# An attention and MoE chain on one core: the order in which weight units are converted, and how many by the end of the attention

## The chip, the cores and the metric

The kernel runs on one core of a Trainium2 chip. Its engines are TensorE (PE, matrix products; its weight loads are shown apart as PEld), VectorE (DVE), ScalarE (ACT), GpSimd (POOL) and SyncE (SP), which here issues the transfers. Each takes its instructions in the order of its own queue. The metric is the time of one execution on the device, in microseconds.

## The reference

A local attention with a few global keys, and then two feed-forward layers ("MoE" by name, with a single expert each) on its output, all in fp32:

```python
scores = scale * (q @ k.T) + bias          # 2 batches x 8 heads, 768 tokens, head size 64
a = softmax(where(keep, scores, -1e9))     # keep: 8 global keys, 96 local ones behind each token
x = (a @ v) as 1536 tokens x 512
h = x @ w_in                               # 512 -> 2048
y = (h * tanh(softplus(h))) @ w_out        # 2048 -> 512
h2 = y @ w2_in
out = softplus(h2) @ w2_out
```

## The kernel before

**Products in two parts.** A factor of a MoE product is held as two float32r tiles, a rounded one and the rest, and a product takes three passes: rounded with rounded, rounded with rest, rest with rounded. The weights arrive as 64-bit words. One **unit** is half a weight tile: 128 partitions x 512 words. A transfer on SP brings its raw words (0.5 MB, `fetch`, line 194), three DVE instructions of `widen` make fp32 of them (lines 145, 150 and 154, into a buffer `a`, with a PSUM bank `bits` between), ACT casts that to the rounded part (line 209), and POOL subtracts it from `a` for the rest (line 211). Unit part 0 of tile n holds the columns that the up product of chunk n needs, part 1 the rows for its down product. There are 16 tiles of a layer, so 64 units in two layers; `raw` and `a` have two buffers each, and the fetch of unit u+2 is issued behind the widening of unit u.

**The order of units** is the list `units` (line 173). Per layer it runs over the tiles: part 0 of tile f, then part 1 of tile f-3 (`SKEW`). Units 10, 11, 12 and 13 so are the second half of tile 3, the first of 7, the second of 4 and the first of 8. The first seven tiles (`EARLY`) live in pool `wa`, which is there from the start; tiles 7 to 14 live in `wb`, which is opened at line 347 behind the attention and lies over memory that the attention's tiles held. A unit of tile 7 can be cast only when these have been read for the last time.

**The attention** works in 24 steps (two query tiles of two heads each): scores on PE (`sp`, line 462), scores with bias and their maximum on DVE (481), exponentials on ACT (492), a small scaling of the sums on POOL (501), the reciprocal on DVE (503), normalisation on POOL (506), transposes on PE (522) and their copies on ACT or DVE (525), products with the values on PE (`xhalf`, 539), and the split of the result into x on ACT and DVE (553, 554). Between scaling and reciprocal, `norm` calls `fill(goal)`, which moves the conversion on; the goal rises evenly to 4 x `PRE` quarter units by the last step.

**The MoE part** counts chunks s = 0 to 95: 2 layers x 3 blocks of 512 tokens x 16 tiles. `up(s)` is 12 matmuls into a PSUM bank `h` (line 247); `chunk(s, goal)` puts the activation on ACT and DVE (lines 102 to 115 in the first layer), splits the result into `g` (ACT 282, POOL 283) and calls `fill(goal)`; `down(s)` is 12 matmuls into the four banks `yp` (line 267), three chunks behind `up`. The chunks 0 to 3 (`AHEAD`) have their up product and activation inside the attention already (`early`). From chunk 4 on the goal of conversion is 4 x `PRE` + `RATE1` x (s - 3) quarter units, until the first layer's 32 units are done. The second layer's units are due by `RATE2`, much later.

The framework's scheduler turns this into the queues of the engines: it keeps pinned instructions (those of `widen`, among others) in the order written and may move the others, so the names and places below are read from the queues that it built. In them a0, a1, ... are the units' buffers, w0 to w15 the weight tiles, h, e, t and g those of a chunk, p, m, z, t, pt and x those of an attention step; the numbers behind an underscore are buffer numbers.

Of the kernel before, what the change touches and what calls it, by code (L numbers as in the profile page):

```python
# [30 lines left out]
FC = DFF // P  # L31
# [4 lines left out]
WMIN2 = float((np.array([0x38100000], np.int32).view(np.float32) ** 2)[0])  # L36
CUTS = ((0, P + NK, 0, 2 * P), (P + NK, P + 3 * NK, 2 * P, 4 * P), (P + 3 * NK, KX, 4 * P, S))
SKEW = 3
PRE = 10
EARLY = 7  # L40
DLAG = 3
LAG = 2
AHEAD = 4
FROM = 15
HPO = 60
RATE1 = 8.0
RATE2 = 4.5
WEIGH = ((14, 1.2, 24), (65, 1.45, 40))

# [2 lines left out]
def moe_chain(ctx, tc, qT, kx, vx, nn, w1, w2, out):  # L52
# [18 lines left out]
    def load_flag(low):  # L71
# [22 lines left out]
        )  # L94

    general = fast_path(tc, small, qT, kx, vx, w1, w2, out, wf[:, 0, 0:1], wf[:, 1, 0:1], two, load_flag)
    with tc.If(general == 1):  # L97
        general_path(tc, qT, kx, vx, w1, w2, out, ng, nl, two)
# [60 lines left out]
def fast_path(tc, small, qT, kx, vx, w1, w2, out, ng, nl, two, load_flag):  # L159
    nc = tc.nc  # L160
    far_side = bass.opposite_side(tc.default_side)
    with ExitStack() as outer:
# [8 lines left out]
        raw = {}  # L171

        units = []
        for n in range(0, 2 * FC, FC):
            for f in range(FC + SKEW):
                units += [(n + f, 0)] if f < FC else []
                units += [(n + f - SKEW, 1)] if f >= SKEW else []

        turns = []
        for i in range(2):  # L180
# [172 lines left out]
        for s in range(DLAG, NS + DLAG):  # L353
# [6 lines left out]
            if AHEAD <= s < NS:  # L360
                up(s)
                r = s - (NB - 1) * FC
                goal = 4 * PRE + int(RATE1 * (s + 1 - AHEAD))
                if goal > 8 * FC:
# [12 lines left out]
def attention(tc, qT, kx, vx, ng, nl, x, fetch, fill, early):  # L377
    nc = tc.nc
    with ExitStack() as st:
# [119 lines left out]
        def norm(i, goal):  # L499
            p, z = prob[i], psums.pop(i)  # L500
            nc.gpsimd.tensor_scalar(out=z, in0=z, scalar1=1e-9, scalar2=1.0, op0=ALU.add, op1=ALU.mult)
            fill(goal)
            nc.vector.reciprocal(z, z)  # L503
            for c in range(4):
                w, _, _ = geom(steps[i][2] + c // 2)
                nc.gpsimd.tensor_scalar(  # L506
                    out=p[:, c, :w],
                    in0=p[:, c, :w],
                    scalar1=z[:, c : c + 1],
                    scalar2=1.0,  # L510
                    op0=ALU.mult,
                    op1=ALU.mult,
                )
# [42 lines left out]
        for i in range(n + LAG + 3):  # L556
# [8 lines left out]
            if 0 <= i - 1 < n:  # L565
                norm(i - 1, 4 * PRE * max(0, i - 2) // (n - 2))
            for e in exps[:2]:
# [194 lines left out]
```

## Time and profile before

| | |
|---|---|
| median of three timed runs | 649.25 us (648.32 to 1016.29) |
| profiled execution | 647.7 us, span from first to last instruction 645.9 us |
| PE busy | 614.1 us, 95% of the span, 3026 matmuls |
| PE weight loads busy | 488.3 us, 76% |
| DVE busy | 481.5 us, 75% |
| ACT busy | 344.0 us, 53% |
| POOL busy | 267.0 us, 41% |
| from HBM | 81.30 MB read |

A row in order of time gives the start, the length, the engine, the source line, what is written from what, and how many like instructions were merged; brackets give idle time ahead of it and what ended that. The ends of matmuls are modelled, so busy time of PE can hide that they come slower than they could. A wait for several things is put down to the last of them. One run of the three took 1016.29 us and is no measure of the kernel.

### The profile page before, as it was taken

The page shows a single profiled execution, that of the slowest core. Times are in us where ns is not written, and L with a number is a line of the kernel's source. Part 1 is how long each engine was busy: PE and PEld are TensorE (multiplying, and loading weights), DVE is VectorE, ACT ScalarE, POOL GpSimd, SP SyncE. Part 2 cuts the span into 40 slices and gives each one's busy share as a digit, 9 for nine tenths or more (in the row PEclk, how much of TensorE's full clock was granted, in tenths as well). Part 3 has the DMA queues.
Part 4 walks back from the last instruction along what each step waited for, and adds up shares of the span by engine and source line. Part 5 has one row for each costly group of instructions (what it writes and reads, how often), then busy time and mean ns, then how long its engine had stood idle before and what let it go on. Part 6 is the DMA issues. An engine that isn't in the chain of part 4 may idle for free. (4 is left out here: it accounts for less than half of the span.)

```text
span 645.9 us, 9028 instructions
## 1 busy us (share of the span) xinstructions
PE 614.1 (95%) x3026; PEld 488.3 (76%) x3026; DVE 481.5 (75%) x998; ACT 344.0 (53%) x715; POOL 267.0 (41%) x297
## 2 busy tenths in 40 slices
PE   5999897969999999999999999999999999999994
PEld 3666675856678888888888888888888888888883
DVE  4788888089999775656897998988778865756642
ACT  4779886155545544444555665555554444444441
POOL 5566666146654232222553554654523222132221
PEclk9999799979999999999999999999999999999998
DMA  8747513035555353431342432432445544644301
GB/s 287 231 166 280 199 48 112 21 97 157 163 170 164 129 162 100 130 98 65 90 135 70 128 101 70 142 114 71 128 142 180 165 131 131 227 132 130 131 1 71
DMA packets 24390, 85.11 MB, mean 132 GB/s; under 512 B 2832, under 2 KB 3600, under 8 KB 24336
## 3 DMA queue, kind: packets, MB, share of 16 engines
q1 hardware_dynamic: 24336, 84.46, 40.7%
q8 instruction: 26, 0.43, 0.3%
q14 instruction: 28, 0.23, 0.1%
HBM read 81.30 MB, written 3.15 MB: 131 GB/s over the span
## 5 line engine op out<-in xcount | busy, mean ns | idle before, releaser
L283 POOL TENSOR_TENSOR g<-e,g 128x512 fp32r<-128x512 f32 x96 | 131.0, 1365 | 256.2 <-ACT g L282 250.5
L247 PE MATMUL h<-x,w 128*128 128x512 f32 x576 | 146.6, 399 | 3.5 <-POOL w L211 2.2
L267 PE MATMUL yp<-g,w 128*128 128x512 f32 x576 | 142.5, 397 | 6.5 <-ACT w L209 5.5
L267 PE MATMUL yp<-w,g 128*128 128x512 f32 x576 | 139.6, 390 | 1.3 <-POOLq L97 0.7
L247 PE MATMUL h<-y,w 128*128 128x512 f32 x576 | 139.2, 390 | 0.0
L267 PEld LDWEIGHTS yp<-g,w 128*128 128x128 f32 x576 | 108.8, 191 | 33.1 <-ACT w L209 6.7
L247 PEld LDWEIGHTS h<-x,w 128*128 128x128 f32 x576 | 108.2, 191 | 30.8 <-POOL w L211 4.6
L267 PEld LDWEIGHTS yp<-w,g 128*128 128x128 f32 x576 | 107.8, 188 | 25.1 <-POOLq L97 1.1
L247 PEld LDWEIGHTS h<-y,w 128*128 128x128 f32 x576 | 108.1, 188 | 22.8
L211 POOL TENSOR_TENSOR w<-a,w 128x512 fp32r<-128x512 f32 x64 | 84.6, 1322 | 74.4 <-ACT w L209 73.7
L282 ACT CAST g<-e 128x512 fp32r<-128x512 f32 x96 | 59.4, 618 | 48.6 <-PE yp L267 44.4
L209 ACT CAST w<-a 128x512 fp32r<-128x512 f32 x64 | 39.6, 619 | 42.5 <-DVE a L154 42.1
L127 DVE SCALAR_TENSOR_TENSOR h<-h,t 128x512 f32<-128x512 f32 x48 | 33.5, 697 | 35.5 <-ACT t L125 35.4
L107 ACT ACTIVATE t<-e,two 128x512 f32<-128x512 f32 x48 | 34.7, 725 | 43.2 <-DVE e L106 43.2
L119 ACT ACTIVATE e<-h 128x512 f32<-128x512 f32 x48 | 28.5, 594 | 43.8 <-PE h L247 33.6
L102 ACT ACTIVATE e<-h 128x512 f32<-128x512 f32 x48 | 28.4, 596 | 41.9 <-PE h L247 28.9
L492 ACT ACTIVATE p<-p,m 128x232 f32<-128x232 f32 (+1 forms) x96 | 44.5, 466 | 11.3 <-DVE m L481 11.1
L115 DVE TENSOR_TENSOR e<-h,t 128x512 f32<-128x512 f32 x48 | 33.0, 687 | 23.0 <-ACT t L110 22.4
L506 POOL TENSOR_SCALAR p<-p,z 128x232 f32<-128x232 f32 (+1 forms) x96 | 42.5, 461 | 15.8 <-DVE z L503 14.6
L125 ACT ACTIVATE t<-t 128x512 f32<-128x512 f32 x48 | 30.3, 631 | 34.9 <-DVE e L124 34.8
L315 DVE CUSTOM_DVE_ANT_0 top<-top 128x512 f32<-128x512 f32 x64 | 47.9, 767 | 0.0
L145 DVE TENSOR_SCALAR bits<-raw 128x512 int32<-128x512 int32 x64 | 44.0, 688 | 4.7 <-DMA raw<-w 4.3
(64 smaller groups left out, 633.8 us busy)
## 6 DMA issues: line engine op xcount, KB each, us to landing
raw<-w SPq DMA_DIRECT2D x64, 512.0 KB, 3.5
top<-w SPq DMA_DIRECT2D x64, 512.0 KB, 3.6
v<-vx SPq DMA_DIRECT2D x8, 704.0 KB, 5.9
k<-kx SPq DMA_DIRECT2D x7, 644.0 KB, 3.8
out<-o SPq DMA_DIRECT2D x12, 256.0 KB, 3.6
q<-qT SPq DMA_DIRECT2D x7, 384.0 KB, 4.4
k<-kx SPq DMA_DIRECT2D x2, 232.0 KB, 3.6
q<-qT SPq DMA_DIRECT2D x3, 128.0 KB, 3.7
```

The lines of the kernel that those rows point to most:

```text
L107: nc.scalar.activation(t, e, AF.Ln, bias=two)
L127: nc.vector.scalar_tensor_tensor(out=h, in0=h, scalar=0.0, in1=t, op0=ALU.max, op1=ALU.add)
L145: nc.vector.tensor_scalar(out=t, in0=top, scalar1=3, scalar2=0x3FFFFFF8, op0=ALU.logical_shift_left, op1=ALU.bitwise_and)
L209: nc.scalar.copy(w[:, 0, half], a)
L211: nc.gpsimd.tensor_tensor(out=w[:, 1, half], in0=a, in1=w[:, 0, half].bitcast(F32), op=ALU.subtract)
L247: nc.tensor.matmul(h, w[:, a, c * P : (c + 1) * P], src[:, c, b, :], start=(n == 0), stop=(n == 3 * CC - 1))
L267: ins = nc.tensor.matmul(yp[s // FC][c], lhsT, rhs, start=(f == 0 and a + b == 0), stop=(f == FC - 1 and b == 1))
L282: nc.scalar.copy(gg[:, 0, :], e)
L283: nc.gpsimd.tensor_tensor(out=gg[:, 1, :], in0=e, in1=gg[:, 0, :].bitcast(F32), op=ALU.subtract)
L315: nc.vector.tensor_tensor_reduce(out=top, in0=top, in1=top, scale=-1.0, scalar=-3.0e38, op0=ALU.mult, op1=ALU.max, accum_out=lows[:, u : u ...
L492: lambda c=c, w=w: nc.scalar.activation(p[:, c, :w], p[:, c, :w], AF.Exp, bias=m[:, c : c + 1], scale=-1.0, accum_out=z[:, c : c + 1])
L506: nc.gpsimd.tensor_scalar(out=p[:, c, :w], in0=p[:, c, :w], scalar1=z[:, c : c + 1], scalar2=1.0, op0=ALU.mult, op1=ALU.mult,)
```

## The change

Two constants and the order of the list change. The list now takes the tiles in three groups, 0 to 6, 7 to 15 and 16 to 31, each staggered by three for itself, so that all 14 units of the first seven tiles come first. `PRE` rises from 10 to 14, so that the goal by the end of the attention is these 14 units, and `RATE1` falls from 8 to 7 quarter units a chunk.

```diff
--- before.py
+++ after.py
@@ -36,14 +36,14 @@
 WMIN2 = float((np.array([0x38100000], np.int32).view(np.float32) ** 2)[0])
 CUTS = ((0, P + NK, 0, 2 * P), (P + NK, P + 3 * NK, 2 * P, 4 * P), (P + 3 * NK, KX, 4 * P, S))
 SKEW = 3
-PRE = 10
+PRE = 14
 EARLY = 7
 DLAG = 3
 LAG = 2
 AHEAD = 4
 FROM = 15
 HPO = 60
-RATE1 = 8.0
+RATE1 = 7.0
 RATE2 = 4.5
 WEIGH = ((14, 1.2, 24), (65, 1.45, 40))
 
@@ -171,10 +171,10 @@
         raw = {}
 
         units = []
-        for n in range(0, 2 * FC, FC):
-            for f in range(FC + SKEW):
-                units += [(n + f, 0)] if f < FC else []
-                units += [(n + f - SKEW, 1)] if f >= SKEW else []
+        for first, last in ((0, EARLY), (EARLY, FC), (FC, 2 * FC)):
+            for n in range(first, last + SKEW):
+                units += [(n, 0)] if n < last else []
+                units += [(n - SKEW, 1)] if n - SKEW >= first else []
 
         turns = []
         for i in range(2):
```

What each engine does for a unit is the same as before, and so is the number of units. Units 10 to 13 now are the second halves of tiles 3, 4, 5 and 6; 14 and 15 are the first halves of tiles 7 and 8. The second layer's units keep their order.

ACT's queue at the end of the attention, before (casts of units 10, 11 and 12):

```order
L209 CAST w3_659<-a10_1515 128x512
L525 COPY pt23_0_1423<-t23_0_1418 116x512
L553 CAST x1_82<-xhalf_123 128x256
L553 CAST x2_83<-xhalf_123 128x256
L209 CAST w7_1531<-a11_1524 128x512
L553 CAST x2_83<-xhalf_123 128x256
L282 CAST g4_1512<-e4_1503 128x512
L102 ACTIVATE e5_1563<-h5_1550 128x512
L102 ACTIVATE e6_1619<-h6_1606 128x512
L107 ACTIVATE t5_1564<-e5_1563,two_61 128x512
L107 ACTIVATE t6_1620<-e6_1619,two_61 128x512
L110 ACTIVATE t5_1564<-t5_1564 128x512
L110 ACTIVATE t6_1620<-t6_1620 128x512
L282 CAST g5_1572<-e5_1563 128x512
L102 ACTIVATE e7_1675<-h7_1662 128x512
L209 CAST w4_860<-a12_1575 128x512
```

and now (casts of units 13, 14 and 15):

```order
L209 CAST w6_1085<-a13_1386 128x512
L553 CAST x2_83<-xhalf_123 128x256
L525 COPY pt22_1_1444<-t22_1_1439 116x512
L553 CAST x1_82<-xhalf_123 128x256
L525 COPY pt23_0_1459<-t23_0_1454 116x512
L553 CAST x2_83<-xhalf_123 128x256
L209 CAST w7_1558<-a14_1551 128x512
L209 CAST w8_1568<-a15_1561 128x512
L553 CAST x2_83<-xhalf_123 128x256
L102 ACTIVATE e5_1599<-h5_1586 128x512
L282 CAST g4_1548<-e4_1539 128x512
```

The cast that completes tile 4 stood behind the activations of chunks 5, 6 and 7. Now tiles 4, 5 and 6 are complete ahead of the last copies of the attention, the casts into tiles 7 and 8 follow, and the split of chunk 4 stands behind the first activation of chunk 5.

DVE's queue in the last steps of the attention, from the end of unit 9 to the last copy of a transpose, before:

```order
L154 SCALAR_TENSOR_TENSOR a9_1349<-raw9_1177,bits9_1350 128x512
L145 TENSOR_SCALAR bits10_1516<-raw10_1300 128x512
L503 RECIPROCAL z23_1343<-z23_1343 128x4
L554 TENSOR_TENSOR x2_83<-xhalf_123,x2_83 128x256
L525 COPY pt22_0_1401<-t22_0_1396 116x512
L150 SCALAR_TENSOR_TENSOR bits10_1516<-raw10_1300,bits10_1516 128x512
L154 SCALAR_TENSOR_TENSOR a10_1515<-raw10_1300,bits10_1516 128x512
L554 TENSOR_TENSOR x2_83<-xhalf_123,x2_83 128x256
L145 TENSOR_SCALAR bits11_1525<-raw11_1386 128x512
L150 SCALAR_TENSOR_TENSOR bits11_1525<-raw11_1386,bits11_1525 128x512
L154 SCALAR_TENSOR_TENSOR a11_1524<-raw11_1386,bits11_1525 128x512
L525 COPY pt23_1_1430<-t23_1_1425 116x512
```

and now, from the end of unit 13 to the same copy:

```order
L154 SCALAR_TENSOR_TENSOR a13_1386<-raw13_1260,bits13_1387 128x512
L525 COPY pt22_0_1437<-t22_0_1432 116x512
L145 TENSOR_SCALAR bits14_1552<-raw14_1382 128x512
L503 RECIPROCAL z23_1375<-z23_1375 128x4
L554 TENSOR_TENSOR x2_83<-xhalf_123,x2_83 128x256
L150 SCALAR_TENSOR_TENSOR bits14_1552<-raw14_1382,bits14_1552 128x512
L154 SCALAR_TENSOR_TENSOR a14_1551<-raw14_1382,bits14_1552 128x512
L145 TENSOR_SCALAR bits15_1562<-raw15_1423 128x512
L150 SCALAR_TENSOR_TENSOR bits15_1562<-raw15_1423,bits15_1562 128x512
L554 TENSOR_TENSOR x1_82<-xhalf_123,x1_82 128x256
L154 SCALAR_TENSOR_TENSOR a15_1561<-raw15_1423,bits15_1562 128x512
L525 COPY pt23_1_1466<-t23_1_1461 116x512
```

Two whole units stand ahead of this copy in both pieces; they were units 10 and 11 and are 14 and 15 now.

PE's queue, before, with chunk 6 among the last products of the attention:

```order
L539 MATMUL xhalf_123<-pt21_0_1363,v7_1211 64x128 x2
L539 MATMUL xhalf_123<-pt21_1_1370,v7_1211 64x128 x4
L247 MATMUL h6_1606<-x0_81,w6_1388 128x512 x10
L522 MATMUL t23_0_1418<-ident_155,p23_1341 116x128 x4
```

and now, with chunk 6 behind the scores of step 21 (the two rows of `sp`):

```order
L522 MATMUL t19_1_1278<-ident_155,p19_1123 116x128 x4
L462 MATMUL sp_124<-k7_1002,q7_1003 128x128 x2
L462 MATMUL sp_124<-k7_1002,q7_1003 128x232 x2
L247 MATMUL h6_1638<-x0_81,w6_1085 128x512 x12
L539 MATMUL xhalf_123<-pt18_0_1223,v6_1041 64x128 x2
L539 MATMUL xhalf_123<-pt18_1_1230,v6_1041 64x128 x4
```

Chunk 6 moved ahead by some two steps of the attention; behind the last product of the attention there now stand 21 down matmuls, chunk 5, the rest of the down products 0 to 3, chunk 7 and down product 4.

## Rows read from the trace of the kernel before

**Rows 1.** The page: span, and TensorE's granted clock in 40 slices, in tenths
```profile
span 645.9 us, 9028 instructions
...
PEclk9999799979999999999999999999999999999998
```

**Rows 2.** PE in order of time: start, us, instructions, idle time before and its end
```profile
112.92 4.90 PE L267 MATMUL yp<-g,w 128*128 128x512 f32 x20 [0.51 <-ACT x L553]
117.75 1.09 PE L539 MATMUL xhalf<-pt,v 116*64 116x128 f32 x16
...
125.06 2.88 PE L247 MATMUL h<-x,w 128*128 128x512 f32 x12
...
128.01 2.88 PE L247 MATMUL h<-x,w 128*128 128x512 f32 x12
135.99 5.16 PE L267 MATMUL yp<-g,w 128*128 128x512 f32 x12 [5.10 <-ACT w L209]
140.98 2.92 PE L247 MATMUL h<-x,w 128*128 128x512 f32 x12
```

**Rows 3.** PE's waits over the span: waited for, us in total, times, longest
```profile
PE yp L267 <- ACT w L209: 5.5, 2, 5.1
...
PE h L247 <- POOL w L211: 2.2, 5, 0.5
```

**Rows 4.** DVE in order of time, at the end of the attention
```profile
110.45 0.69 DVE L154 SCALAR_TENSOR_TENSOR a<-raw,bits 128x512 int32<-128x512 int32 x1
...
128.61 0.92 DVE L104 TENSOR_SCALAR t<-e 128x512 f32<-128x512 f32 x2 [7.72 <-ACT e L102]
...
134.57 0.69 DVE L154 SCALAR_TENSOR_TENSOR a<-raw,bits 128x512 int32<-128x512 int32 x1
```

**Rows 5.** ACT in order of time, the two weight casts there
```profile
119.54 0.62 ACT L209 CAST w<-a 128x512 fp32r<-128x512 f32 x1 [0.28 <-ACT x L553]
...
135.33 0.61 ACT L209 CAST w<-a 128x512 fp32r<-128x512 f32 x1
```

**Rows 6.** Four stretches: busy us and instructions of each engine, clock, DMA
```profile
20.00:60.00 40.00, 38.42 (x338) 26.23 (x334) 32.18 (x132) 32.39 (x116) 26.81 (x59) 1.00 0.64 218
60.00:113.00 53.00, 46.51 (x359) 33.89 (x357) 44.74 (x142) 41.48 (x126) 34.01 (x60) 0.94 0.40 132
141.00:185.60 44.60, 41.49 (x169) 30.42 (x168) 41.31 (x68) 24.32 (x41) 26.82 (x21) 1.00 0.51 157
185.60:229.40 43.80, 43.80 (x193) 36.06 (x192) 38.24 (x66) 23.48 (x40) 17.64 (x13) 1.00 0.52 156
```

**Rows 7.** The instructions of one weight unit: busy us, mean ns of one
```profile
L211 POOL TENSOR_TENSOR w<-a,w 128x512 fp32r<-128x512 f32 x64 | 84.6, 1322 | 74.4 <-ACT w L209 73.7 <-DVE z L503 0.3
...
L150 DVE SCALAR_TENSOR_TENSOR bits<-raw,bits 128x512 int32<-128x512 int32 x64 | 44.1, 690 | 0.9
L145 DVE TENSOR_SCALAR bits<-raw 128x512 int32<-128x512 int32 x64 | 44.0, 688 | 4.7 <-DMA raw<-w 4.3
L154 DVE SCALAR_TENSOR_TENSOR a<-raw,bits 128x512 int32<-128x512 int32 x64 | 43.5, 680 | 1.5
...
L209 ACT CAST w<-a 128x512 fp32r<-128x512 f32 x64 | 39.6, 619 | 42.5 <-DVE a L154 42.1 <-ACT x L553 0.3
```

**Rows 8.** DVE's waits from 10 to 113 us
```profile
DVE z L503 <- POOL z L501: 10.0, 8, 2.8
```

**Rows 9.** PE in order of time: gaps in the attention
```profile
70.27 1.09 PE L539 MATMUL xhalf<-pt,v 116*64 116x128 f32 x16 [1.07 <-DVE x L554]
72.73 1.57 PE L462 MATMUL sp<-k,q 64*128 64x128 f32 x8 [1.37 <-DVE m L481]
74.23 5.31 PE L247 MATMUL h<-x,w 128*128 128x512 f32 x12
...
98.78 0.67 PE L522 MATMUL t<-ident,p 128*128 128x128 f32 x2 [1.17 <-POOL p L506]
...
103.89 1.09 PE L539 MATMUL xhalf<-pt,v 116*64 116x128 f32 x16 [1.73 <-DVE x L554]
```

## The prediction

> **What bounds the kernel now.** I read the page first: TensorE (PE) is busy 95% of a span of 645.9 us [rows 1], so time can only be won where PE stands still or runs slowly. The row of granted clock shows two weak places, slices 5 and 9 of forty (16.1 us each): around 74 us, inside the attention, and around 135 us, after it. Then I read PE in order of time around the second place. The down products of the first MoE tiles begin at 112.92 us, the last attention product (xhalf) stands at 117.75 behind 20 of them, and from 130.89 (128.01 + 2.88) to 135.99 PE does nothing; the twelve matmuls after that take until 140.98, 4.99 us [rows 2]. The waits name the cause: a down product waited 5.1 us for a cast on ScalarE (ACT) into a weight tile [rows 3]. The reader is to see in VectorE (DVE) and ACT why that cast was late: DVE ends unit 11 at 111.14 and then does little until 128.61, since the next row in its queue is the activation of a chunk that PE reaches only at 125.06 [rows 2]; unit 12 is finished at 135.26, and ACT's cast at 135.33 follows at once [rows 4, 5]. Unit 12 is the second half of tile 4, and it is the tile that PE needs. Unit 11, which took the place before, is the first half of tile 7: it was ready at 111.14, but its buffer lies over the attention's memory and its cast ran only at 119.54, when nobody needed it yet [rows 4, 5].
>
> Last come the stretches. From 185.6 to 229.4 us PE runs 193 matmuls in 43.8 us, 0.227 us each, 2.72 us for the twelve of a chunk: that is its full pace here. From 141 to 185.6 it runs 169 in 44.6 us, 6.3 to 6.5 us too slow (169 x 0.227 = 38.1), while DVE is busy 41.31 of 44.6 us [rows 6]. These are seven steps of an up and a down product, 6.4 us each instead of 5.44; conversion at two units a step is the bound.
>
> **What of this goes.** (a) The wait: down product 4 needs the second half of tile 4, which is unit 11 now and is cast before the attention's last copies. Likewise 12 and 13 complete tiles 5 and 6. So 5.1 us go. (b) The slow product after it: 4.99 - 2.72 = 2.3 us [rows 2]. (c) The slow stage: after the attention 16 units are left (two of them widened already) instead of 20, at 7/4 units a step instead of 2. Work on DVE per step is 41.31/7 = 5.9 us now; a quarter of a unit less (a unit is three DVE instructions of 0.69 us, 2.06 us [rows 7]) makes 5.4 us, PE's own 5.44. And PE begins with a lead. By the new order it runs four down products, chunks 5 and 7 and down product 4 from the attention's end on: 84 matmuls, 19.1 us, all with weights that are there, since tiles 7 and 8 are cast right at the attention's end. Then come chunk 8, down product 5 and, 24.5 us after the end, chunk 9. Its tile (unit 16) waits on ACT behind the first activation of chunk 7, which PE ends 16.3 us after the end; with a cast of 0.62 and a POOL subtraction of 1.32 [rows 7] and a little queueing it is there at some 19 us, 5.5 us early. What is late next is then nothing on PE: (c) gives 6.5 us. Sum: 13.9 us.
>
> PE's idle time in the same stretch, 44.6 - 41.49, is only 3.1 us [rows 6]. The busy time of the weight loads says more: 30.42 of 44.6 us, where the full pace has 36.06 of 43.8, so 30.42 would fit into 36.9, a loss of 7.6. The Trainium skill (Perfetto Trace Analysis, Identifying the Most-Contended Engine) calls matmul busy time a bad measure of how close TensorE is to its limit and takes the share of weight loads instead; by matmul busy time my net result below would be 5.8 us, by the loads 10.3. The count of matmuls, 6.5, is what I use.
>
> **What it costs.** (d) DVE's order holds 16 units ahead of the last copy of the attention instead of 12, so four more units lie in it: 4 x 2.06 = 8.2 us of DVE, and three or four casts of 0.62 and subtractions of 1.32 [rows 7]. Four more weight loads of 0.5 MB move into that stretch too, on SP's queue between the loads of keys and values. DVE waited 4.3 us for raw data over all 64 units [rows 7], 0.07 us each, so I cost four more at nothing; the two raw buffers are their cover, and if it went the whole 4.3 us could move in here. From below the price of the units is nothing: DVE is idle 40 - 32.18 = 7.8 us from 20 to 60 and 53 - 44.74 = 8.3 us from 60 to 113 [rows 6], of which 10.0 us are waits at the reciprocal for POOL's short scaling [rows 8], and a unit placed ahead of such a wait fills it. From above it is 8.2, if DVE sets the attention's pace. I take 3.5: of the first stretch's 3.5 us (1.7 units) nothing, since PE is busy 38.42 of 40 there and DVE has twice the room; of the second's 4.7 us (2.3 units) three quarters, since DVE is busy 84% there and PE, idle 6.5 us, waits for it. The last 11 us, from the last scores to the last product, hold three units in both orders, so the tail doesn't grow. (e) Chunk 6 is moved from this tail to a place between the scores of steps 21 and 22. PE's work is the same, but the tail has fewer matmuls to fill its gaps. Around 70 us two such gaps (1.07 and 1.37 us) came before twelve matmuls that took 5.31 us, at a granted clock of 0.7 in that slice; between 98 and 104 gaps of 1.17 and 1.73 left it at 0.9 or more [rows 1, 9]. So the first down products may run at 1.2 GHz or at 2.4: nothing, or the 2.3 to 2.6 us that the two slow groups lost. One row stands for each, and I take half, 1.2.
>
> ACT now has the exponential of chunk 5 ahead of the split of chunk 4, which waits with it until PE has run 21 down matmuls and chunk 5, some 7.5 us; down product 4 comes 16.3 us after the end, so this is hidden by some 7 us. The second layer's units keep their order and their due steps, and from 185.6 us on PE runs at full pace: what is won there shifts the rest whole.
>
> Net: 13.9 - 3.5 - 1.2 = 9.2 us. The profiled execution is at 647.7 us with a span of 645.9; the median of the three timed runs is 649.25, 1.55 above it. So I expect a span of 636.7 and a median of 640.0.
>
> **The rivals.** A, all hidden: the four units fit into DVE's waits and the clock stays up. For it speak 16 us of idle DVE against 8.2; against it that DVE works in order, so that a unit fills only the gap behind it. 13.9 less: 635.3 us.
> B, the attention pays in full: DVE sets its pace, 8.2 us, and the clock falls, 2.3. For it speaks that PE's weight loads are busy only 33.89 of 53 us there [rows 6], against it the 10 us of waits for POOL. 13.9 - 10.5 = 3.4 less: 645.9 us. The page just named speaks for this one, as it would not call TensorE full at that share.
> C, conversion goes on as the bound: the stage after the attention keeps its 6.4 us a step, since 5.4 us of DVE in 5.44 leaves it no room for a late weight load. Against it stand the 5.5 us of lead. (c) is not won: 13.9 - 6.5 - 4.7 = 2.7 less, 646.6 us.
> D, slower: in the softmax loop each added unit stands in series, its DVE part ahead of a score reduction or reciprocal and its POOL part ahead of a normalisation that PE's transposes wait for. Then a unit costs 2.06 + 0.62 + 1.32 = 4.0 us, four 16.0, against 13.9: 651.4 us. It decides from 3.5 us a unit on. Against it: POOL is idle 19 of 53 us there [rows 6], and casts run while DVE goes on.
> That the change doesn't do what it says I leave out: the new order shows all fourteen units cast ahead of the last copies.
>
> **How the numbers follow.** Forecast 0.52, A 0.18, B 0.13, C 0.13, D 0.04. The prediction is the forecast's 640.0; the range, 634.5 to 647.0, reaches from A to B and C and leaves out D and what goes beyond A. About 2% is what a measurement of this kernel can tell from no change; 2% under 649.25 is 636.3, so only A is faster by that: 0.18. D ends within 2% and would need more than its price to pass 662: 0.01 slower, 0.81 within.
>
> **What would show it.** Right: no wait of PE for a weight cast near the attention's end; some 4.4 matmuls a us from there on, DVE busy below 90% in the first 20 us of it; the last attention product ending about 3 to 4 us later than 114 (112.92 and its own 1.09). Wrong: this product at 122 or later (B, D), PE's waits for POOL's subtraction into weights as long as now, 2.2 us in five [rows 3] (C), or a new wait for tile 7 or 8 behind the attention's end.

## The result and the profile after

The changed kernel takes 639.9 us in the median of four runs (638.66 to 640.52) against 649.1 for the kernel before in the same comparison: a ratio of 0.986, 95% interval 0.984 to 0.988, 9.2 us less. The profiled execution is at 639.5 us with a span of 637.7, 8.2 us under the span of before.

The page of the changed kernel, span and granted clock [rows 1]:

```profile
span 637.7 us, 9026 instructions
...
PEclk9899999999999999999999999999999999999999
```

The two weak slices of before, 5 and 9, are full; only slice 2 (16 to 32 us) is a little low. PE in order of time, from the end of the attention to the last chunk of the first layer's first block [rows 2]; columns as there:

```profile
115.69 0.66 PE L539 MATMUL xhalf<-pt,v 116*64 116x128 f32 x8 [1.36 <-DVE x L554]
116.80 0.66 PE L539 MATMUL xhalf<-pt,v 116*64 116x128 f32 x8 [0.45 <-DVE pt L525]
117.39 7.00 PE L267 MATMUL yp<-g,w 128*128 128x512 f32 x29
124.22 2.90 PE L247 MATMUL h<-x,w 128*128 128x512 f32 x12
126.97 4.47 PE L267 MATMUL yp<-g,w 128*128 128x512 f32 x19
131.27 2.88 PE L247 MATMUL h<-x,w 128*128 128x512 f32 x12
...
166.75 2.88 PE L267 MATMUL yp<-g,w 128*128 128x512 f32 x12
170.45 0.73 PE L247 MATMUL h<-x,w 128*128 128x512 f32 x2 [0.82 <-ACT w L209]
171.81 2.56 PE L247 MATMUL h<-x,w 128*128 128x512 f32 x10 [0.62 <-POOL w L211]
175.06 1.19 PE L267 MATMUL yp<-g,w 128*128 128x512 f32 x4 [0.69 <-ACT w L209]
176.43 2.12 PE L267 MATMUL yp<-g,w 128*128 128x512 f32 x8 [0.18 <-POOL w L211]
178.38 5.70 PE L247 MATMUL h<-x,w 128*128 128x512 f32 x24
```

The last attention product ends and the MoE part takes over at 117.39 us; I call this the **hand-over**. Before, the same work is done at 113.95 (112.92, plus the 1.03 us of the product that stands behind twenty down products there [rows 2]). So the attention lasts 3.44 us longer. From the hand-over PE runs at its full pace up to 169.5 us, with no wait where there were 5.1 us; then it waits four times for weights, 2.3 us together, around the up product of chunk 14. Counted in matmuls, 252 of them lie between the hand-over and the up product of chunk 15 and take 57.1 us at full pace. Before they took 71.7 us (113.95 to 185.6), now 61.0 (117.39 to 178.38): the loss fell from 14.5 to 3.9 us. 10.6 won and 3.4 paid is 7.2; the last matmuls end 7.6 us earlier and the span 8.2. The remaining 0.6 us lies in the last drains and was not followed up.

VectorE (DVE) around the hand-over [rows 4], and the stretches of the changed kernel (PE, PEld, DVE, ACT, POOL: busy us and instructions; clock; DMA) [rows 6]:

```profile
113.80 0.69 DVE L145 TENSOR_SCALAR bits<-raw 128x512 int32<-128x512 int32 x1 [0.36 <-DMA raw<-w]
...
115.46 0.68 DVE L154 SCALAR_TENSOR_TENSOR a<-raw,bits 128x512 int32<-128x512 int32 x1
116.06 0.68 DVE L525 COPY pt<-t 116x512 f32<-116x512 f32 x1
...
127.80 0.43 DVE L104 TENSOR_SCALAR t<-e 128x512 f32<-128x512 f32 x1 [7.75 <-ACT e L102]
```

```profile
60.00:113.00 53.00, 47.75 (x398) 34.12 (x394) 49.69 (x157) 44.90 (x139) 37.61 (x68) 1.00 0.48 159
117.40:133.70 16.30, 16.30 (x73) 13.41 (x72) 5.67 (x10) 5.48 (x10) 5.12 (x4) 1.00 0.08 29
133.70:169.60 35.90, 35.90 (x158) 29.23 (x157) 35.58 (x54) 20.34 (x35) 20.01 (x15) 1.00 0.44 132
```

Unit 15, the sixteenth, is done at 116.14, just ahead of the attention's last copy. Then DVE is idle for 7.75 us in front of the activation of chunk 5 (L104), as long as before (7.72 [rows 4]): the next unit again stands behind it, but now PE doesn't need it yet. From 133.7 on DVE is busy 35.58 of 35.9 us while PE keeps its pace; that is where the lead is used up. In the attention DVE's wait at the reciprocal for POOL's scaling has shrunk to 4.7 us in three [rows 8: 10.0 in eight], filled by the added units.

### The profile page after: what moved, and what is told of

Its sections match the earlier page's. It is cut to its first block, busy times and chain, and to the rows that moved or that the text cites. A ratio compares the mean times of both kernels' runs of the same rounds, so it can differ in the third digit from the quotient of the medians.

```text
span 637.7 us, 9026 instructions
## 1 busy us (share of the span) xinstructions
PE 610.0 (96%) x3026; PEld 488.5 (77%) x3026; DVE 485.0 (76%) x998; ACT 343.4 (54%) x715; POOL 266.8 (42%) x297
## 5 line engine op out<-in xcount | busy, mean ns | idle before, releaser
L247 PE MATMUL h<-x,w 128*128 128x512 f32 x576 | 143.0, 395 | 2.1 <-ACT w L209 0.8
L267 PE MATMUL yp<-g,w 128*128 128x512 f32 x576 | 139.1, 390 | 0.9 <-ACT w L209 0.7
L115 DVE TENSOR_TENSOR e<-h,t 128x512 f32<-128x512 f32 x48 | 33.0, 687 | 25.7 <-ACT t L110 25.5
L106 DVE SCALAR_TENSOR_TENSOR e<-e,t 128x512 f32<-128x512 f32 x48 | 44.3, 925 | 2.4
```

Source lines behind the costliest of these rows:

```text
L106: nc.vector.scalar_tensor_tensor(out=e, in0=e, scalar=ECLAMP, in1=t, op0=ALU.min, op1=ALU.mult)
L247: nc.tensor.matmul(h, w[:, a, c * P : (c + 1) * P], src[:, c, b, :], start=(n == 0), stop=(n == 3 * CC - 1))
L267: ins = nc.tensor.matmul(yp[s // FC][c], lhsT, rhs, start=(f == 0 and a + b == 0), stop=(f == FC - 1 and b == 1))
```

## The experiments

Line numbers of experiments with inserted lines are shifted by 1 to 10. Each time is a median, each difference is against runs of the kernel before on the same chip.

**Two units exchanged, nothing else.** Before, unit 12 (the missing half of tile 4) came behind unit 11 (first half of tile 7), which nobody needed yet; here they change places.

```diff
+        units[11], units[12] = units[12], units[11]
```

> The kernel before with units 11 and 12 exchanged in the list (second half of tile 4 ahead of the first half of tile 7), nothing else. Theory (unit 12 was late because it stood behind a unit that must wait for the attention's memory and behind the activations of chunks 5 to 7): the wait for the cast into tile 4 and the slow product behind it go, 7.4 us, the attention ends where it did (113 to 115 us) and the time is 641 to 643 us. Rival (DVE is what lacks time behind the attention, whatever unit comes first): the 5.1 us turn up as a wait for tile 7 or 8, and the time stays at 647 to 650 us.

650.2 us, ratio 1.003 (1.002 to 1.005): nothing won. PE and then DVE:

```profile
128.20 3.11 PE L268 MATMUL yp<-g,w 128*128 128x512 f32 x13
136.43 1.22 PE L248 MATMUL h<-x,w 128*128 128x512 f32 x2 [5.12 <-ACT w L210]
```

```profile
110.91 0.69 DVE L154 SCALAR_TENSOR_TENSOR a<-raw,bits 128x512 int32<-128x512 int32 x1
...
129.08 0.91 DVE L104 TENSOR_SCALAR t<-e 128x512 f32<-128x512 f32 x2 [8.05 <-ACT e L102]
...
133.12 0.68 DVE L145 TENSOR_SCALAR bits<-raw 128x512 int32<-128x512 int32 x1
```

The wait is as long as before (5.12 against 5.10 us [rows 2]), only at the up product of chunk 7 and for tile 7. Twelve units are done by 111 us, and the thirteenth, whichever it is, begins at 133 behind the activations of chunks 5 and 6. My theory fell, the rival held.

**The order alone.** The changed kernel with the two constants put back.

```diff
-PRE = 14
+PRE = 10
-RATE1 = 7.0
+RATE1 = 8.0
```

> The changed kernel with PRE back at 10 and RATE1 back at 8, so that only the order of the list is changed. Theory (the wait of 5.1 us and the slow product of 2.3 us hang on the order alone, the attention's extra 3.4 us on the number of units): the last attention product ends at 113 to 115 us in the trace, PE waits nowhere over 2 us for a cast into tile 4, and the time is about 7 us under the kernel before, 641 to 644 us, less a late tile 7. Rival (the number of units done by the end of the attention is what counts): the wait stays at about 5 us, only at another tile, and the time is within 2 us of the kernel before.

656.8 us, ratio 1.013 (1.012 to 1.015): 8.5 us slower than before. PE waits twice, for the thirteenth unit, now the second half of tile 5, and for the seventeenth, the first half of tile 9, whose widening stands behind the activation of chunk 7 (DVE waits 3.98 us for that one):

```profile
136.46 8.05 PE L267 MATMUL yp<-g,w 128*128 128x512 f32 x24 [5.12 <-ACT w L209]
...
156.12 1.22 PE L247 MATMUL h<-x,w 128*128 128x512 f32 x2 [6.17 <-ACT w L209]
```

The rival's wait came, but its time was too good: the order by itself does harm, since it puts tiles 7 to 9 last. The reverse, fourteen units in the old order, was not tried: unit 11 of the old order belongs to tile 7, and its pool `wb` is opened only behind the attention. `RATE1` by itself was not varied either. The order makes room for the number of units; the number is what pays.

**Two of the four units.**

```diff
-PRE = 14
+PRE = 12
```

> The changed kernel with PRE at 12. Fourteen units, not sixteen, then stand ahead of the last copies of the attention on DVE, and the fifteenth, the first half of tile 7, behind the activation of chunk 5. Theory now (whatever unit is the first behind the hand-over is converted only after the activations of chunks 5 and 6, at some 129 us; the wait goes only if PE doesn't need that unit before some 137 us): chunk 7 is the first to need it, 48 matmuls and chunk 5 behind the attention's end, so PE stands 4 to 6 us at the up product of chunk 7, and the time is 646 to 650 us. Rival (each unit more by the end of the attention brings its share, half of the gain of 9 us for two units of four): no wait over 2 us, and 643 to 645 us.

644.8 us, ratio 0.993 (0.991 to 0.994), 4.6 us less than before: the time is the rival's, half the gain for half the units, but the waits are the theory's kind. PE stands for the split of chunk 5 (the scheduler puts the activations of chunks 5 and 6 together again, as before) and for a bank of `h`; 1.23 and 1.85 us for a weight follow at 161.89 and 164.47:

```profile
130.79 7.08 PE L267 MATMUL yp<-g,w 128*128 128x512 f32 x24 [2.78 <-ACT g L282]
...
148.89 3.02 PE L247 MATMUL h<-x,w 128*128 128x512 f32 x12 [2.86 <-DVE e L115]
```

**The kernel before, with units in DVE's idle time.** Neither order nor number changed; one call of `fill` ahead of the MoE loop.

```diff
+        fill(4 * PRE + 16)
         weighed = 0
         for s in range(DLAG, NS + DLAG):
```

> The kernel before, order and number of units by the end of the attention as they were, with one call of fill, to 4 x PRE + 16 quarter units, between the attention and the MoE loop. Units 10 to 13 then stand on DVE behind the attention's last copy and ahead of the activation of chunk 5. Theory (before, the thirteenth unit was late only because it stood behind that activation while DVE was idle for 7.7 us): the wait of 5.1 us for the cast into tile 4 and the slow product behind it go without a unit more in the attention, which ends at 112 to 114.5 us; DVE stays the bound afterwards, two units a step, so that little of the slow stage is won: 639 to 643 us. Rival (the attention's memory, and not DVE's queue, holds the cast of tile 7 and with it all that follows): a wait of 3 us or more remains, and 645 to 650 us.

645.1 us, ratio 0.994 (0.992 to 0.995), 4.2 us less. On DVE units 10, 11 and 12 stand between the attention and chunk 5, unit 13 begins beside its activation:

```profile
118.29 0.68 DVE L145 TENSOR_SCALAR bits<-raw 128x512 int32<-128x512 int32 x1
120.46 0.69 DVE L145 TENSOR_SCALAR bits<-raw 128x512 int32<-128x512 int32 x1
124.12 0.70 DVE L145 TENSOR_SCALAR bits<-raw 128x512 int32<-128x512 int32 x1 [1.45 <-DMA raw<-w]
126.26 0.76 DVE L104 TENSOR_SCALAR t<-e 128x512 f32<-128x512 f32 x2
126.93 0.69 DVE L145 TENSOR_SCALAR bits<-raw 128x512 int32<-128x512 int32 x1
```

The 5.1 us wait is gone without a unit more in the attention, as the theory said, but the time is not the theory's: PE now loses it in small pieces, 2.21 us at 145.87 the largest. By these rows the wait was the first place where DVE's lag showed, and not a loss of its own. Two units more by 128 us brought 4.2 us, and two units more brought 4.6 us with PRE at 12: about their own DVE time, 2 x 2.06 us [rows 7].

**DVE's work behind the hand-over cut.** Units 16 to 27 of the changed kernel with one instruction instead of three (diff: `widen` called only for the other units, else its first instruction alone, writing `a`).

> The changed kernel, with the units 16 to 27 widened by one DVE instruction instead of three, which leaves out two thirds of their work on DVE (12 x 1.37 = 16.4 us) and gives weights that are wrong. Theory (the 3.9 us that PE loses between 169 and 178 us come from DVE, which is 99% busy from 134 us on): the 3.9 us go, the up product of chunk 15 begins about 61 - 3.9 = 57 us behind the last attention product, and the time is about 636 us. Rival (the chain cast, subtraction, weight load or the attention's memory makes tile 14 late): the 3.9 us stay, 639 to 640 us.

636.9 us, ratio 0.984 (0.981 to 0.986). No row of PE between 115 and 190 us carries a wait; chunk 15 begins at 173.47, where the changed kernel with the same attention (the run "a second time", below) has 177.13. So 3.7 of the 3.9 us are DVE's. The same cut on units 10 to 13, inside the attention, was to show that DVE is what made the attention longer:

> The changed kernel, with the units 10 to 13 widened by one DVE instruction instead of three, which leaves out 4 x 1.37 = 5.5 us of DVE's work inside the attention and gives weights that are wrong. Theory (the added units' time on DVE is what made the attention 3.4 us longer, partly in its last 3 us): the last attention product ends 1.5 to 3.5 us earlier than the 117.4 us of the changed kernel and the time falls by as much, to 636.5 to 638.5 us. Rival (ACT's casts, POOL's subtractions or the moved up product of chunk 6 made it longer): it ends within 0.7 us of 117.4, and the time stays at 639 to 640 us.

639.7 us, ratio 0.989 (0.986 to 0.991): nothing won, a miss. The hand-over is at 115.52, 1.9 us earlier, but TensorE's clock fell at other places in this execution (74 to 78 and 111.5 to 115.5 us, against 27 to 34), so that the two ends can't be compared; the stall behind is the same, and a wait of 1.47 us near 469 us that the changed kernel has not took most of the rest.

**The changed kernel a second time.**

> The changed kernel as it is, a second time. Theory (TensorE's spells at 1.2 GHz fall at other places from execution to execution, since kernels with the same attention showed them at 27 to 34, 25 to 29 and 74 to 78 us): the time is again 638.5 to 641 us, the loss of some 3.9 us between chunk 14 and chunk 15 is there again, and the spells stand elsewhere, which moves the attention's end by up to 2 us. Rival (the place of the spells is fixed by the program): the same spell at 27 to 34 us and the attention's end within 0.3 us of 117.4.

639.3 us, ratio 0.986 (0.984 to 0.988). The same program, with TensorE at 1.2 GHz elsewhere (a granted clock of about 0.5 in these stretches), first in the first execution, then twice in the second:

```profile
27.00:34.00 7.00, 6.68 (x29) 4.29 (x30) 2.64 (x14) 3.13 (x14) 2.15 (x6) 0.51 0.68 275
```

```profile
25.00:29.00 4.00, 3.94 (x22) 2.54 (x22) 1.79 (x11) 3.55 (x14) 1.39 (x4) 0.57 0.93 347
114.00:117.50 3.50, 3.45 (x14) 2.65 (x15) 0.60 (x2) 1.78 (x4) 0.92 (x1) 0.51 0.49 152
```

In the second the hand-over is at 115.10 instead of 117.39, and the 29 down products behind it take 8.05 us instead of 7.00:

```profile
112.94 0.66 PE L539 MATMUL xhalf<-pt,v 116*64 116x128 f32 x8 [1.28 <-DVE x L554]
114.05 1.12 PE L539 MATMUL xhalf<-pt,v 116*64 116x128 f32 x8 [0.45 <-DVE pt L525]
115.10 8.05 PE L267 MATMUL yp<-g,w 128*128 128x512 f32 x29
```

**POOL's subtractions out of DVE's way.** The page of lines shows what DVE spent in its full stretch, 133.7 to 169.6 us: the two instructions of an activation that have their operands in SBUF alone, L106 and L104, are the only ones that are longer than before. Mean ns in the column behind the bar and the comma; first the changed kernel, then before from 141 to 185.6 us:

```profile
L106 DVE SCALAR_TENSOR_TENSOR e<-e,t 128x512 f32<-128x512 f32 x7 | 8.2, 1168 | 0.0
...
L104 DVE TENSOR_SCALAR t<-e 128x512 f32<-128x512 f32 x6 | 4.2, 708 | 0.0
```

```profile
L106 DVE SCALAR_TENSOR_TENSOR e<-e,t 128x512 f32<-128x512 f32 x7 | 5.4, 777 | 0.0
...
L104 DVE TENSOR_SCALAR t<-e 128x512 f32<-128x512 f32 x7 | 3.4, 491 | 0.4 <-ACT e L102 0.2
```

Beside POOL they read so, DVE and then POOL of the changed kernel:

```profile
148.74 1.67 DVE L106 SCALAR_TENSOR_TENSOR e<-e,t 128x512 f32<-128x512 f32 x1
...
154.37 0.68 DVE L106 SCALAR_TENSOR_TENSOR e<-e,t 128x512 f32<-128x512 f32 x1
```

```profile
148.56 1.30 POOL L283 TENSOR_TENSOR g<-e,g 128x512 fp32r<-128x512 f32 x1 [0.63 <-ACT g L282]
...
155.19 1.29 POOL L211 TENSOR_TENSOR w<-a,w 128x512 fp32r<-128x512 f32 x1 [2.14 <-ACT w L209]
```

The L106 at 148.74 meets a subtraction and ends 0.55 us behind it; the one at 154.37 runs between two (the one before ends at 153.05) and takes 0.68. To test it, POOL's subtractions of that stage went:

```diff
-                nc.gpsimd.tensor_tensor(out=w[:, 1, half], ...)
+                if 16 <= u < 28:
+                    nc.scalar.copy(w[:, 1, half], a)
+                else:
+                    nc.gpsimd.tensor_tensor(out=w[:, 1, half], ...)
...
-            nc.gpsimd.tensor_tensor(out=gg[:, 1, :], ...)
+            if 5 <= s < 15:
+                nc.scalar.copy(gg[:, 1, :], e)
+            else:
+                nc.gpsimd.tensor_tensor(out=gg[:, 1, :], ...)
```

> The changed kernel, with POOL's subtractions of the units 16 to 27 and of the chunks 5 to 14 left out; ACT writes a plain second cast in their place (0.62 us each), so the rest tiles of these factors are wrong. DVE's work and order stay. In the changed kernel DVE's two instructions of an activation, L104 and L106, took 0.42 and 0.68 us where POOL was idle and up to 1.12 and 1.67 us where they met a subtraction, 0.71 and 1.17 us in the mean between 133.7 and 169.6 us. Theory (that is what made DVE fall behind by some 0.6 us a step and used up PE's lead): they take 0.42 to 0.50 and 0.68 to 0.75 us in that stretch, PE loses under 1.5 us between 169 and 178 us instead of 2.3 us of waits and 3.9 us in all, and the time is 635 to 638 us. Rival (DVE is too slow at three instructions a unit whatever POOL does): the waits stay, and the time is 639 to 641 us; if ACT, with 1.2 us more a step, becomes late itself, weights wait for its casts and the time is 640 us or more.

637.4 us, ratio 0.982 (0.980 to 0.984). In the same stretch:

```profile
L106 DVE SCALAR_TENSOR_TENSOR e<-e,t 128x512 f32<-128x512 f32 x7 | 4.8, 684 | 0.0
L104 DVE TENSOR_SCALAR t<-e 128x512 f32<-128x512 f32 x8 | 3.3, 418 | 0.0
```

PE has no wait between the hand-over and 190 us, although ACT did 29.62 us of work in 35.9 where it had 20.34. So POOL's subtractions made the stall. A shorter chain behind DVE is not the reason: the rest tile that chunk 14 needs was there 2.0 us behind its widening in the changed kernel (169.75 to 171.75) and 2.2 us here (167.88 to 170.09). But POOL did not make all of DVE's load, which is busy 33.83 of the 35.9 us without the subtractions too, and the collisions alone did not use up the lead. Unit 16, which chunk 9 needs, and unit 25, which chunk 14 needs, get their last widening instruction at these times, first in the changed kernel, then without the subtractions:

```profile
133.94 0.68 DVE L154 SCALAR_TENSOR_TENSOR a<-raw,bits 128x512 int32<-128x512 int32 x1
...
169.07 0.68 DVE L154 SCALAR_TENSOR_TENSOR a<-raw,bits 128x512 int32<-128x512 int32 x1
```

```profile
135.07 0.68 DVE L154 SCALAR_TENSOR_TENSOR a<-raw,bits 128x512 int32<-128x512 int32 x1
...
167.20 0.68 DVE L154 SCALAR_TENSOR_TENSOR a<-raw,bits 128x512 int32<-128x512 int32 x1
```

From the one to the other DVE took 35.1 us and then 32.1, while PE's five steps from chunk 9 to chunk 14 take 27.2. So some 3 us of that are the collisions.

**Better than both: units 14 to 17 in the idle time.** The changed kernel with the same call of `fill` as above; units 14 and 15 leave the attention's tail, and 16 and 17 come ahead of chunk 5.

> The changed kernel with one more call of fill, to 4 x PRE + 16 quarter units, between the attention and the MoE loop. Units 14 to 17 then stand on DVE behind the attention's last copy and ahead of the activation of chunk 5, where DVE was idle for 7.75 us. Theory: the copy comes 1 to 2 us earlier, and two units more are done before DVE's full stretch begins at 134 us, 4.1 us of its work, which covers the 3.9 us that PE lost between 169 and 178 us: 3 to 5.5 us less than the changed kernel, 634.5 to 637 us. Rival (units 14 and 15 now come too late for chunks 7 and 8, or the activation of chunk 5 now waits behind the units and with it the down products): a new wait near 130 us, and 639 to 643 us.

635.9 us, ratio 0.981 (0.979 to 0.983), 3.4 us under the changed kernel on the same chip. The gap of 1.36 us ahead of the last product is gone, and of the four waits two are left:

```profile
110.55 0.66 PE L540 MATMUL xhalf<-pt,v 116*64 116x128 f32 x8
111.41 0.66 PE L540 MATMUL xhalf<-pt,v 116*64 116x128 f32 x8 [0.20 <-DVE pt L526]
111.99 6.54 PE L267 MATMUL yp<-g,w 128*128 128x512 f32 x27
...
170.55 0.72 PE L247 MATMUL h<-x,w 128*128 128x512 f32 x2 [0.99 <-ACT w L209]
171.91 3.75 PE L247 MATMUL h<-x,w 128*128 128x512 f32 x15 [0.65 <-POOL w L211]
```

This execution shows full clock from 10 to 190 us, which makes its hand-over look better than the change in the code alone. A part of the 3.4 us goes with the clock as well: the timed runs with a mean granted clock of 0.991 read 637.0 us here and 639.3 and 639.7 for the changed kernel, 2.2 to 2.6 us apart. Whether the smaller gaps are why the spells are fewer stays open. Six units instead of four:

> The changed kernel with the call of fill between the attention and the MoE loop, now to 4 x PRE + 24 quarter units: units 14 to 19 behind the attention's last copy and ahead of the activation of chunk 5, six where the run with + 16 had four. Theory (each unit that DVE does ahead of its full stretch saves its own 2.06 us there, until PE is the bound): the 2.5 us that PE still lost behind the hand-over with four units go, and the time is 633 to 635.5 us. Rival (the activation of chunk 5 now waits behind the raw data of the units 18 and 19, and down product 5 waits for it): a wait of 1.5 us or more of a down product near 134 us, and 636 to 639 us.

633.7 us, ratio 0.978 (0.977 to 0.979), the fastest kernel here. One wait of PE for weights is left behind the hand-over, 0.4 us. Unit 18 begins at 127.17 instead of 131.84, in a gap of chunk 5's activation. And the same number of units ahead of chunk 5 with two fewer in the attention:

> The same with PRE at 12: units 0 to 11 inside the attention, as many as the kernel before has ahead of its hand-over, and units 12 to 17 behind its last copy and ahead of the activation of chunk 5; 18 units stand ahead of that activation, as in the run with PRE 14 and + 16. Theory (what counts is how many units are done ahead of DVE's full stretch, and two units inside the attention cost PE about 1 us): the attention ends 0.5 to 2 us earlier than with PRE 14, nothing waits over 2 us behind it, and the time is within 2 us of the run with PRE 14 and + 16, 634 to 638 us. Rival (six units in series with their raw data don't fit into DVE's idle time there, so tile 7 and the activation of chunk 5 come late): waits of 2 us or more near 130 us, and 639 to 645 us.

639.3 us, ratio 0.987 (0.985 to 0.988): a miss in the time. The attention's work ends at 110.98 (109.96 plus 1.02), 1.0 us earlier, as expected, and the activation of chunk 5 wasn't late. But the scheduler puts 23 down products ahead of the last attention product again (at 115.50 us), so DVE gets its last input late and begins with unit 12 at 118.25 where the run with four units began at 113.72; units 16 and 17 fall behind the activation.

**All of them together.** Units begun on DVE by 128 us, and the difference to the kernel before:

| kernel | units by 128 us | us against before |
|---|---|---|
| before | 12 | 0 |
| 11 and 12 exchanged | 12 | +1.9 |
| before, with `fill` | 14 | -4.2 |
| changed, PRE 12 | 14 | -4.6 |
| changed | 16 | -9.2, -10.1 |
| changed, PRE 12, `fill` 24 | 16 | -8.8 |
| changed, `fill` 16 | 18 | -13.5 |
| changed, `fill` 24 | 19 | -14.4 |

From 12 to 18 units each is worth 2.2 us net (13.5 / 6), near the 2.06 us that it takes on DVE, whatever the place that it is moved to; then PE's own pace is reached, 14.5 us being all that PE lost before. This is a count and not a test of its own, and the clock has a share in it: the median runs of the last two rows have a mean clock of 0.995 and 0.994, the changed kernel 0.991, before 0.989. Only the order alone (12 units, +8.5) stands outside, with its second wait.

## Why the prediction was right, and where it was not

The forecast was a span of 636.7 and a median of 640.0; they are 637.7 and 639.9. By the trace the terms give 10.6 - 3.4 = 7.2 us where the forecast had 9.2; two of them, (c) and (e), were wrong and cancel in part. That the median agrees to 0.1 us is luck: the span is 1.0 us off, and the offset between span and median, carried over as 3.35 us (649.25 - 645.9), is 2.2 now.

**(a) and (b), the wait of 5.1 us and the slow product of 2.3 us: gone, the reason half wrong.** I put the late unit 12 down to its neighbour of tile 7 and to its place behind the activations of chunks 5 to 7. The second is right (DVE idle 7.7 to 8.1 us in front of L104 in every kernel with 12 units). The first is not: exchanging the two moved the wait and left its length, and the new order alone cost 8.5 us. It was the number of units ahead of the activation, which the order only makes possible.

**(c), the slow stage, 6.5 us: mis-sized by 3.3.** The whole loss fell by 10.6 us, where (a), (b) and (c) together had 13.9. The lead at chunk 9 was worked out nearly rightly: unit 16 was cast at 135.16 and subtracted by 137.29, 4.9 us ahead of chunk 9's up product at 142.15 (forecast: 5.5). The failed step is the work of DVE per step, put at 5.4 us for an activation and 7/4 units, against PE's own 5.44, so that the lead would last. It failed twice.

It took the length of DVE's instructions as fixed. With DVE full, L106 and L104 met POOL's subtractions more often and grew by 0.39 and 0.22 us; an activation of DVE followed the last one after 5.9 us (L109 at 138.96 and, five chunks on, at 168.47) instead of 5.4 without the subtractions (139.59 to 166.60). With them away the stall was away too. The Trainium skill (SBUF — State Buffer, Who interferes with whom) has the rule: VectorE and GpSimd share a pair of SBUF ports, and a VectorE instruction with two SBUF inputs, or in a mode that uses both ports, blocks while a GpSimd instruction that reads SBUF holds them. The rows agree: L106 has two inputs in SBUF, and L109 and L115, which read one of theirs (`h`) from PSUM, stay at 0.68 us in all three kernels. L104 has one input, and no run here shows the mode that it runs in.

And it took 7/4 units a chunk from the goal in the code. By that goal unit 25 is widened behind the activation of chunk 10. In DVE's queue, with and without the subtractions, it ends behind all of chunk 11's and three of the four instructions of chunk 12's: nine units, 17 to 25, stand among 25 instructions of activations, 1.44 units a chunk. Nine units at 7/4 a step of 5.4 us are 27.8 us. DVE took 35.1, and PE came to chunk 14 after 27.3, so the lead was gone there. Of the 7.3 us too many, some 3 are the collisions; the rest is this order and short waits of DVE, and no run tried another order there. Rival C named the right place, a DVE with no room; half of its price, 3.3 of 6.5 us, was paid.

**(d), the attention, 3.5 us: 3.44 by the first trace of the changed kernel, 1.15 by the second (115.10 - 113.95), and for partly another reason.** That 3.44 meets the forecast is luck. I let three quarters of the late units pay and said that the tail doesn't grow. It does: unit 15 stands ahead of the last copy with 0.36 us of waiting for its raw data, the copy came at 116.06 though PE's transposes were done at 114.3 (113.18 + 1.15), and PE waited for it. From the gap for POOL (109.00 us; 105.29 with `fill` 16) to the hand-over the changed kernel takes 8.39 us and the one with units 14 and 15 behind the copy 6.70: 1.7 us are the tail. The two units between PRE 12 and 14 cost 1.0 us. The spells of low clock fell elsewhere in each trace, so 3.44 has an error of some 2 us, and that DVE's time is what the units inside cost was not shown (the run with four short units is inconclusive). Raw data for four more units cost little, as said: DVE waited 0.7 us for it up to 117 us. Rival B's 8.2 us and D's 16 are excluded.

**(e), the clock at the hand-over, 1.2 us: not paid in the profiled execution, 1.5 in the next.** The granted clock stayed at 1.00 from 113 to 125 us in the first and fell in the second: 1.05 us on the down products and 0.46 on the last attention product. Of four executions with this attention three paid: these 29 down products took 8.05 us in the second, 7.98 with the late units short and 8.34 without POOL's subtractions, with a granted clock of 0.5 in a part of them, against 7.00 in the first. So half of the price was a fair term, rather low.

**Later.** The split of chunk 4 began on ACT at 128.75, 11.4 us behind the hand-over and not some 7.5 (29 down products, not 21, ran ahead of chunk 5); it stayed hidden, since down product 4 came at 133.99. Nothing behind chunk 15 took the gain back in the changed kernel. Rival A failed by (c) and (d).

## What to carry to other kernels

Where engines work in order, don't ask which piece of work is late but how much of it is queued ahead of the first instruction that waits for another engine: exchanging two units moved a wait of 5.1 us and left its length, two more units ahead took 4.2 to 4.6 us off the time. Idle time in front of such an instruction (7.7 us here) is the cheapest place for more: one call moved two units there and two out of a tail, and won 3.4 us. Count the pieces in the queue as it was built, not by the rate in the code: 7/4 units a chunk there were 1.44 in DVE's queue. And the length of an instruction is not a constant when a stage gets denser: take it from the stage that is as full as the one you forecast, and look for a partner engine that it collides with.

## What the runs showed of the hardware

A collision of DVE with POOL shows as longer instructions, not as a wait: 0.68 us became up to 1.67 and 0.42 up to 1.12, and DVE counted as 99% busy. POOL's instructions grew too: a subtraction of 1.30 us took 1.75 where it began at 167.36 beside an L106 that ran until 167.95. It is told from work by comparing one line's mean between stretches (777 and 1168 ns).

The same program had TensorE at 1.2 GHz from 27 to 34 us in one execution and from 25 to 29 and 114 to 117.5 us in another; four other kernels show full clock all through the attention. The same two gaps, 1.28 to 1.36 and 0.45 us, came before a fall in one execution and before none in the other. Why the clock falls in one and not in the other stays open. A hand-over read from one trace is uncertain by some 2 us, as much as a unit is worth.
